# Two groups of resident blocks set one chunk earlier, and the rows ahead of their lists cleared

## The chip, the core and the metric

The kernel runs on one core of a Trainium2 chip. The metric is the time of one execution on the device in microseconds (us). The engines named here are PE (TensorE, matrix products), ACT (ScalarE), DVE (VectorE), POOL (GpSimd, which issues the indirect transfers here) and SP (SyncE, which issues the other transfers). Each engine works through its own instructions in a fixed order and waits on semaphores.

## The reference

A gated linear recurrence over four sequences of 3648 tokens with 256 features, and then a mixture of 16 experts, in four groups of four, over all 14592 tokens:

```python
a_t = np.exp(c * sig_r * np.log(a_base))           # c = 8
x_gated = sqrt(max(1 - a_t * a_t, 1e-6)) * sig_i * x
for t in range(S):
    h = a_t[:, t] * h + x_gated[:, t]
    y[:, t] = h
...
g_idx = argmax(y @ w_group)                        # the group, and then the expert in it
e_idx = argmax(y @ w_expert[g_idx])
out[tok] = g_w * e_w * (np.maximum(y @ w1[g, e], 0) @ w2[g, e])     # 256 -> 1024 -> 256
```

Each token goes through one expert only.

## The kernel before

**Recurrence and routing.** The tokens are worked off in 16 chunks (`SIZES`: 4, then thirteen times 8, then 4 and 2 tiles of 128 tokens), features on partitions. For each chunk six transfers on SP's queue bring the three inputs (`load`, L251), ACT forms the gates and the decay, DVE scales and scans (L359). PE then turns the chunk into rows and multiplies it with the routers in the same products (`rows1`, L366), and ACT copies them out (`rows2`, L372). DVE finds each token's expert (`route1`, `route3`, `weigh`). PE ranks the tokens within the experts (`rank`, L448 and L449), DVE turns the ranks into row numbers (`route4`), and POOL scatters the rows, with token number and weight beside the features, into a list for each expert in device memory (`scatter`, L469, one transfer for each tile of 128 tokens, into `y_s`). A list has room for `BPE` = 59 times 256 rows, and 384 rows (`HEAD`) lie before its first one. One block of 256 rows behind all lists stands for "nothing", and is cleared near the start by one transfer (`clear`, L313).

**The experts.** They are worked off in four kinds of steps:

- *Resident blocks* (`Block`): experts 0, 4, 8 and 12 (`RES`) have their weights loaded at the start (`load_raw`, L968, 2 MB each in two transfers). After the chunks named in `RSTAGES` (numbered from 0), PE sums the counts (`counts`, L598), and DVE decides for each of the four lists which 128 rows are taken (`near`, L690 to L707): they start at the smaller of (own count - 128) and the number already done; rows that were taken before, or precede the list, are masked. A group is then four blocks of 128 rows (`add_blocks`): a transfer of the rows on SP (`rows_block`, L479), two transposes on PE (`turn_block`, L1026), the masking of the columns on DVE (L485), a copy on ACT (`copy_block`, L1030), and two halves of first products (`mm1_block`, L1037, with `relu_block`, L1042, on ACT) and of second products (`mm2_block`, L1049; in f32 each product is two instructions in the trace, 32 and 16 for a block), then the weighting on DVE (L1054) and a scatter to the output by POOL (L1057).
- *Native units*: full blocks of 256 rows, found after the chunks 4, 7 and 10 (`STAGES`), 26 units in all. The first twelve (`NATIVE`) take their weights as they are, into the four places of the resident weights in turn (`load_native`, L976), and work in plain f32 (L982, L992, L1006).
- *Pair units*: the other units of 256 rows, the last 11 of them found after the last chunk. Their weights are split into two parts by ACT and DVE (L814, L816), and the products are made of three (L861, L930).
- *Tails*: one unit for each expert with the two or three blocks of 128 rows that are left.

Should there be more than 11 pairs after the last chunk, a conditional part at the very end takes the others one by one.

**The order.** Every step is an operation in a plan (`Plan`): engine, assumed cost, due time, what it follows, and the rings of buffers that it takes from. `Plan.run` places the operations on a modelled clock, the earliest first and among those the one that is due first, and emits the instructions in that order. So the order on each engine is fixed when the kernel is built. The due times of a block are those of its chunk plus `ORES` (60) and 7.2 for each block; the first unit's is that of the last of `RSTAGES` plus 60 and four times 7.2 (`first`, L1262); a chunk's due time is 16.5 times its number. A rank of a chunk follows the counts that were taken after the chunk before (`hold`). A transfer that reads rows from `y_s` waits for the scatters that stand before it in the order.

Of the kernel before, what the change touches and what calls it, by code (L numbers as in the profile page):

```python
# [8 lines left out]
F32 = mybir.dt.float32  # L9
# [35 lines left out]
class Plan:  # L45
# [14 lines left out]
    def op(self, engine, cost, emit, due, after=(), new=(), use=(), dma=0, table=None, soon=0.0, order=()):  # L60
        o = Op(engine, cost, emit, due, new, use, dma, table, soon)
        after = dict.fromkeys(a for a in after if a)
        order = dict.fromkeys(a for a in order if a and a not in after)
        o.wait = len(after) + len(order)
        for b in o.new + o.use:
            b.left += 1
        for a in after:
            a.then.append(o)
        for a in order:
            a.next.append(o)  # L70
        self.ops.append(o)
        return o
# [70 lines left out]
def rglru_moe_kernel(ctx: ExitStack, tc: tile.TileContext, x, r_gate, i_gate, a_param,  # L143
                     w_group, w_expert, w1, w2, out):
    nc = tc.nc
    V, S, G, T, DMA = nc.vector, nc.scalar, nc.gpsimd, nc.tensor, nc.sync

    P, NB = 128, 4
# [3 lines left out]
    NE = 16  # L152
# [3 lines left out]
    DW = D + LW  # L156
# [3 lines left out]
    TS = 256  # L160
    BPE = NTOK // TS + 2
    HEAD = 3 * P
# [1 line left out]
    SIZES = [4] + [8] * 13 + [4, 2]   # L164
    CH = 8

    RES, RSTAGES = (0, 4, 8, 12), (2, 3)
    STAGES = [(4, 8), (7, 9), (10, 9)]
    NATIVE = 12

# [1 line left out]
    PBUFS = dict(q_r=2, q_y=1, q_h=2, q_o=1)  # L172
    NA = sum(n for _, n in STAGES)
    NR = len(RES)
    assert NR == 4 and RSTAGES[-1] < STAGES[0][0]

    NP = NT >> 1
    NPS = 37 - NA
# [15 lines left out]
    const = ctx.enter_context(tc.tile_pool(name="const", bufs=1))  # L194
# [4 lines left out]
    rings, pools = {}, {}  # L199
# [13 lines left out]
    y_s = dram.tile([NBLK * TS, DW], F32, name="y_s")  # L213
# [13 lines left out]
    op = plan.op  # L227
# [77 lines left out]
        V.tensor_scalar(tcs[:, k:k + 1], tcol, float(k * P), None, op0=ALU.add)  # L305


    zero = const.tile([P, DW // 2], F32, name="zero")
    V.memset(zero, 0.0)

    def clear(dst):
        k = dst.shape[0] // P
        return DMA.dma_start(dst.rearrange("(p k) (a c) -> p (k a) c", k=k, a=2),  # L313
                             zero.unsqueeze(1).broadcast_to([P, 2 * k, DW // 2]))

    cleared = op("SP", 0.1, lambda: clear(y_s[NE * BPE * TS:, :]), 8.0, dma=5e5, soon=8)

# [1027 lines left out]
```

## Time and profile before

| | us |
|---|---|
| Median of three runs | 957.08 |
| Lowest and highest run | 954.96, 960.32 |
| The profiled execution | 946.03 |
| Its span, first to last instruction | 944.3 |

The profile is of one execution. Its page gives the busy time of each engine and, in 40 equal slices of the span, the busy tenths of each; other views cut the span into given stretches (busy time of each engine, the clock granted to PE, the busy share of the transfer engines), list one engine's instructions in order of time with the idle time before each and what ended it, or sum up who waited for whom. PEld is PE's loading of the stationary operand, which overlaps its products. "SPq" is SP issuing a transfer. Names such as `q_o<-w1l,hh` are the tile that is written and those that are read; weights and rows that share one place share its name.

### The profile page before, as it was taken

Reading aid. Unit: us, or ns where it says so; the run is one execution under the profiler, and the core shown is the slowest. Engines: PE = TensorE matmul, PEld = TensorE weight load, DVE = VectorE, ACT = ScalarE, POOL = GpSimd, SP = SyncE. Lnnn points to the kernel's source line nnn. Section 1 sums busy time; section 2 is a strip of 40 time slices with the busy share of each in tenths; the row PEclk is TensorE's granted clock in tenths of the full one; section 3 lists DMA queues with packets and bytes.
Section 4 is the critical chain, followed back from the end, with each engine's and each line's share of the span. In section 5 each row is a group of like instructions: output and inputs, shape, how many; then the busy total and the mean of one; then the engine's idle time right before and its main releaser. Section 6 shows DMA issues by size and latency. Waiting matters only on the chain. (4 is left out here: it accounts for less than half of the span.)

```text
span 944.3 us, 18467 instructions
## 1 busy us (share of the span) xinstructions
PE 856.5 (91%) x6082; PEld 821.6 (87%) x6082; DVE 620.2 (66%) x1304; ACT 590.5 (63%) x881; POOL 287.0 (30%) x290
## 2 busy tenths in 40 slices
PE   1335889999999999999999999999999999999984
PEld 1235879988989888999999999999999999999984
DVE  3779777675775426677777777777766666575761
ACT  9999889876797324555555555555645555454541
POOL 2244456465643653111111111111111312122222
PEclk9656889999999999999999999999999999999997
DMA  8997777889886756567667767777763657454410
GB/s 318 424 375 247 278 254 265 297 308 393 292 315 242 232 197 207 159 223 235 214 225 225 229 222 225 225 243 255 234 209 130 189 165 229 136 167 155 131 42 21
DMA packets 72456, 215.60 MB, mean 228 GB/s; under 512 B 10504, under 2 KB 28432, under 8 KB 68241
## 3 DMA queue, kind: packets, MB, share of 16 engines
q1 hardware_dynamic: 60464, 183.04, 58.1%
q0 software_dynamic: 11872, 31.10, 8.6%
q8 instruction: 59, 0.97, 0.4%
q14 instruction: 61, 0.49, 0.1%
HBM read 182.76 MB, written 33.43 MB: 229 GB/s over the span
## 5 line engine op out<-in xcount | busy, mean ns | idle before, releaser
L953 POOL DMA_INDIRECT out_dram<-o,cl x122 | 131.7, 1079 | 484.2 <-ACT o L945 286.1
L469 POOL DMA_INDIRECT y_s<-wf,pi x114 | 135.0, 1184 | 112.8 <-issue 71.4
L865 ACT ACTIVATE a<-q_h 128x384 fp32r<-128x384 f32 (+1 forms) x128 | 56.4, 447 | 108.5 <-PE q_h L861 92.8
L861 PE MATMUL q_h<-x,w1h 128*128 128x384 f32 (+1 forms) x512 | 116.1, 316 | 7.4 <-DVE i L868 6.8
L868 DVE SCALAR_TENSOR_TENSOR i<-q_h,a 128x384 fp32r<-128x384 f32 (+1 forms) x128 | 61.7, 497 | 85.3 <-ACT a L865 81.2
L865 ACT ACTIVATE hh<-q_h 128x512 fp32r<-128x512 f32 x100 | 60.3, 603 | 91.1 <-PE q_h L861 80.8
L861 PE MATMUL q_h<-xh,w1h 128*128 128x256 f32 x400 | 113.2, 283 | 0.0
L861 PE MATMUL q_h<-xl,w1h 128*128 128x256 f32 x400 | 112.6, 282 | 0.0
L861 PE MATMUL q_h<-xh,w1l 128*128 128x256 f32 x400 | 112.4, 281 | 0.0
L816 DVE TENSOR_TENSOR w1l<-wf,w1h 128x1024 fp32r<-128x1024 f32 x82 | 99.9, 1222 | 11.8 <-ACT w1h L814 9.8
L868 DVE SCALAR_TENSOR_TENSOR hl<-q_h,hh 128x512 fp32r<-128x512 f32 x100 | 68.9, 689 | 54.3 <-ACT hh L865 54.2
L366 PE MATMUL q_y<-yw,a 128*128 128x148 f32 x368 | 63.3, 318 | 41.2 <-DVE a L359 32.7
L366 PEld LDWEIGHTS q_y<-yw,a 128*128 128x128 f32 x368 | 57.5, 211 | 47.8 <-DVE a L359 18.8
L816 DVE TENSOR_TENSOR w2l<-wf,w2h 128x1024 fp32r<-128x1024 f32 x82 | 98.2, 1219 | 0.0
L861 PEld LDWEIGHTS q_h<-x,w1h 128*128 128x128 f32 x512 | 84.2, 188 | 9.0 <-issue 6.3
L814 ACT CAST w1h<-wf 128x1024 fp32r<-128x1024 f32 x82 | 86.9, 1064 | 0.3 <-issue 0.3
L814 ACT CAST w2h<-wf 128x1024 fp32r<-128x1024 f32 x82 | 83.9, 1043 | 0.0
L861 PE MATMUL q_h<-x,w1l 128*128 128x384 f32 (+1 forms) x256 | 79.7, 311 | 0.0
L861 PEld LDWEIGHTS q_h<-xh,w1h 128*128 128x128 f32 x400 | 75.3, 188 | 0.0
L861 PEld LDWEIGHTS q_h<-xh,w1l 128*128 128x128 f32 x400 | 75.3, 188 | 0.0
L861 PEld LDWEIGHTS q_h<-xl,w1h 128*128 128x128 f32 x400 | 75.2, 188 | 0.0
L359 DVE TENSOR_TENSOR_SCAN a<-a,v 128x1024 f32<-128x1024 f32 (+8 forms) x38 | 67.7, 1796 | 0.1
(341 smaller groups left out, 1930.6 us busy)
## 6 DMA issues: line engine op xcount, KB each, us to landing
wf<-in_moe_w_dram SPq DMA_DIRECT2D x164, 512.0 KB, 4.8
a<-in_r_gate_dram SPq DMA_DIRECT2D x26, 512.0 KB, 10.3
i<-in_i_gate_dram SPq DMA_DIRECT2D x26, 512.0 KB, 9.9
x<-in_x_dram SPq DMA_DIRECT2D x26, 512.0 KB, 8.8
g<-y_s SPq DMA_DIRECT2D x37, 276.0 KB, 4.1
w1h<-in_moe_w_dram SPq DMA_DIRECT2D x8, 1024.0 KB, 7.7
w1l<-in_moe_w_dram SPq DMA_DIRECT2D x8, 1024.0 KB, 9.8
w2h<-in_moe_w_dram SPq DMA_DIRECT2D x8, 1024.0 KB, 9.8
```

What stands on the lines that cost most here:

```text
L359: V.tensor_tensor_scan(a[:, sl], a[:, sl], v[:, sl], init, ALU.mult, ALU.add)
L366: T.matmul(q[:, k, h * P:h * P + YW], lhsT=ck.t["a", h][:, (2 * i + k) * P:(2 * i + k + 1) * P], rhs=yw[:, h, :], start=h == 0, stop=h == ...
L469: ins = G.indirect_dma_start(out=y_s, out_offset=bass.IndirectOffsetOnAxis(ap=ck.pi[:, k:k + 1], axis=0), in_=ck.t["yo", k // 4][:, k % 4, ...
L814: S.copy(hi[m.b][:, sl], src)
L816: V.tensor_tensor(lo[m.b][:, sl], src, hi[m.b][:, sl].bitcast(F32), op=ALU.subtract)
L861: T.matmul(q, lhsT=w[m.b][:, c, fs], rhs=mv[:, c, :N], start=n == 0, stop=n == 5)
L865: S.activation(hh, q, AF.Relu)
L868: V.scalar_tensor_tensor(hl, q, 0.0, hh.bitcast(F32), op0=ALU.max, op1=ALU.subtract)
L953: ins = G.indirect_dma_start(out=out, out_offset=bass.IndirectOffsetOnAxis(ap=m.col("idx", h), axis=0), in_=m.o[h], in_offset=None, bounds ...
```

## The change

The two groups of resident blocks follow the chunks 1 and 2 instead of 2 and 3. A list may now hold fewer than 128 rows when its first block is taken: the block then begins before the list's first row. The 128 rows before the four lists are therefore cleared, too. The zeros no longer have a small tile of their own in `const`, but take one of the two tiles into which units fetch their rows (`g`), for one row of 276 values on each partition; the clearing is now two transfers: one of 256 rows as before, with rows of 1104 bytes instead of halves of 552, and one of 4 x 128 rows. The plan is told 848 thousand bytes for it instead of 500 thousand. The due time of the first unit is taken from the last of `RSTAGES` and so becomes smaller by 16.5.

```diff
-    RES, RSTAGES = (0, 4, 8, 12), (2, 3)
+    RES, RSTAGES = (0, 4, 8, 12), (1, 2)
...
-    assert NR == 4 and RSTAGES[-1] < STAGES[0][0]
+    assert NR == 4 and RES == tuple(range(0, NE, NE // NR)) and RSTAGES[-1] < STAGES[0][0]
...
-    zero = const.tile([P, DW // 2], F32, name="zero")
+    zero = pools["g"].tile([P, 2, DW], F32, name="g")[:, 0:1, :]
     V.memset(zero, 0.0)
 
-    def clear(dst):
-        k = dst.shape[0] // P
-        return DMA.dma_start(dst.rearrange("(p k) (a c) -> p (k a) c", k=k, a=2),
-                             zero.unsqueeze(1).broadcast_to([P, 2 * k, DW // 2]))
-
-    cleared = op("SP", 0.1, lambda: clear(y_s[NE * BPE * TS:, :]), 8.0, dma=5e5, soon=8)
+    def clear():
+        k = TS // P
+        DMA.dma_start(y_s[NE * BPE * TS:, :].rearrange("(p k) c -> p k c", k=k), zero.broadcast_to([P, k, DW]))
+        heads = y_s[0:NE * BPE * TS, :].rearrange("(e r) c -> r e c", e=NR)[HEAD - P:HEAD]
+        DMA.dma_start(heads, zero.broadcast_to([P, NR, DW]))
+
+    cleared = op("SP", 0.1, clear, 8.0, dma=(2 + NR) * P * DW * 4, soon=8)
```

## The prediction

> **What bounds the kernel now.** First the page's shares and its 40 slices: which engine is full, and from when.
>
> ```profile
> span 944.3 us, 18467 instructions
> ...
> PE 856.5 (91%) x6082; PEld 821.6 (87%) x6082; DVE 620.2 (66%) x1304; ACT 590.5 (63%) x881; POOL 287.0 (30%) x290
> ...
> PE   1335889999999999999999999999999999999984
> ...
> ACT  9999889876797324555555555555645555454541
> ```
>
> A slice is 23.6 us. TensorE (PE) is full from the seventh on; before that ScalarE (ACT) is. So I cut the span by stage (columns: stretch, length, busy time and instructions of each engine, granted PE clock, DMA share, GB/s).
>
> ```profile
> 0.00:60.00 60.00, 20.16 (x84) 18.00 (x84) 33.74 (x79) 53.59 (x61) 14.09 (x27) 0.74 0.97 381
> ...
> 60.00:76.00 16.00, 2.17 (x9) 1.57 (x10) 14.41 (x31) 15.93 (x17) 12.26 (x11) 0.60 0.80 277
> 76.00:97.00 21.00, 13.62 (x58) 12.80 (x58) 18.95 (x42) 19.92 (x25) 6.72 (x7) 0.66 0.77 281
> 97.00:140.00 43.00, 37.44 (x233) 33.93 (x232) 31.23 (x94) 36.42 (x46) 22.10 (x23) 0.88 0.75 266
> 140.00:179.20 39.20, 39.13 (x274) 36.79 (x273) 31.48 (x67) 36.78 (x45) 19.51 (x15) 1.00 0.78 267
> 179.20:500.00 320.80, 320.80 (x2071) 297.87 (x2070) 200.35 (x520) 192.06 (x291) 123.81 (x129) 1.00 0.73 251
> 500.00:600.00 100.00, 100.00 (x846) 100.00 (x845) 72.78 (x110) 59.80 (x95) 16.06 (x17) 1.00 0.71 224
> 600.00:900.00 300.00, 293.41 (x2273) 291.67 (x2272) 201.47 (x334) 162.71 (x278) 62.98 (x55) 1.00 0.59 189
> ```
>
> From 140 us to 600 us PE stands idle for 0.07 us, at full clock. A microsecond won before 140 us therefore reaches the end whole, as long as PE never runs out of work behind it; one won on ACT or DMA there reaches it not at all. PE's idle time is 13.83 us in 60:76, 7.38 in 76:97 and 5.56 in 97:140, 26.8 in all.
>
> The timeline of PE shows what stands in these stretches (start, length, operation, count; in brackets the idle time before it).
>
> ```profile
> 54.65 0.22 PE L448 MATMUL q_y<-cn,tri 128*128 128x16 bf16 x1
> ...
> 68.94 0.17 PE L598 MATMUL q_y<-cacc,ones 128*128 128x16 bf16 x1 [2.44 <-DVE cacc L455]
> ...
> 76.73 2.18 PE L366 MATMUL q_o<-yw,a 128*128 128x148 f32 x8
> ...
> 90.78 0.60 PE L1026 MATMUL q_r<-yw,hl 128*128 128x128 f32 x4
> ...
> 97.05 5.54 PE L1037 MATMUL q_h<-xh,w1h 128*128 128x128 f32 x32
> ...
> 126.00 1.17 PE L366 MATMUL q_y<-yw,a 128*128 128x148 f32 x8
> ...
> 145.24 3.73 PE L1037 MATMUL q_h<-xh,w1h 128*128 128x128 f32 x32
> 148.81 1.17 PE L366 MATMUL q_y<-yw,a 128*128 128x148 f32 x8
> 149.82 3.62 PE L1049 MATMUL q_o<-w1l,hh 128*128 128x256 f32 x16
> ...
> 179.19 1.89 PE L992 MATMUL q_h<-xh,w1h 128*128 128x256 f32 x8
> ```
>
> The rank of the second chunk (L448) stands at 54.65, the counts for the first group (L598) at 68.94, behind the third chunk. Its first product (L1037) comes at 97.05; the eight blocks last until the first resident-weight unit (L992) at 179.19. One block is 3.73 + 3.62 = 7.35 us of PE at full clock, the eight 58.8 us.
>
> **The change part by part: the groups move.** The work per group stays the same; each group may begin one chunk sooner. How soon is read from the scatters, for which the row transfers (L479) wait.
>
> ```profile
> 67.30 2.02 POOL L469 DMA_INDIRECT y_s<-wf,pi  x1 [0.30 <-issue]
> ...
> 82.55 1.21 POOL L469 DMA_INDIRECT y_s<-wf,pi  x1 [0.30 <-issue]
> ```
>
> ```profile
> 85.31 1.95 SPq L479 DMA_DIRECT2D hl<-y_s  x2
> ...
> 140.54 1.55 SPq L479 DMA_DIRECT2D g<-y_s  x2
> ...
> 153.81 0.34 SPq L976 DMA_DIRECT2D w1l<-in_moe_w_dram  x1
> ```
>
> The third chunk's last scatter ends at 83.8 and the rows leave at 85.31; the second chunk's ends at 69.3, so its rows can leave at 70.8. From the row transfer to the first product it was 97.05 - 85.31 = 11.7 us before, of which 5.5 to the transposes (L1026); 70.8 + 5.5 is 76.3 for the transposes. PE can have block work from about 76. Nothing of 60:76 can be filled.
>
> How much of 76:97 is? What PE does there now is row products (L366):
>
> ```profile
> 76.00:97.00 21.00, 12.98 (x52) 12.08 (x51) 0.66 0.77 281
> ```
>
> I take the idle share and clock of 97:140, where blocks and row products mix already: 5.56/43 = 13%, clock 0.88. Then 21.0 - 2.7 = 18.3 us are busy; the row products take 12.98 x 0.66/0.88 = 9.7, the rest of what is there (13.62 - 12.98) 0.6. That leaves 8.0 us for blocks, 7.0 us at full clock. In 97:140 the first product ran cold, 5.54 against 3.73 us: with PE busy before it, and fewer such gaps later, I add 2 us. **Sum: 9 us** less between 76 and 179. Its bounds: 0, if no block fits in earlier; and, if every gap from 76 on closes at full clock, 7.38 + 13.62 x 0.34 + 5.56 + 37.44 x 0.12 = 22.1.
>
> The Trainium skill ("TensorE: Matmul & The Clock Gate", Part 1) says PE's clock is halved after an idle window of about 3.4 us and full after a busy one. The trace agrees: a group of eight row products takes 2.18 us at 76.73 and 1.17 at 126.00. By that rule alone all work from 76 on would be at full speed, and the sum would be 18.3 - 12.98 x 0.66 - 0.4 = 9.3 for 76:97 and 37.44 x 0.12 = 4.5 for 97:140, some 14 us.
>
> **Does the work last until unit 0 is ready?** At 179.2 - 9 = 170 the blocks end. Unit 0 needs its row numbers (140.54, where its rows are fetched) and its weights, issued at 153.81 when the first block of the second group let go of its place (149.82 + 3.62).
>
> ```profile
> w1l<-in_moe_w_dram SPq DMA_DIRECT2D x8, 1024.0 KB, 9.8
> ...
> y_s<-zero SPq DMA_DIRECT2D x1, 276.0 KB, 10.9
> ```
>
> They land 9.8 us later; with that block 9 us sooner, at 153.81 - 9 + 9.8 = 155. There are 15 us in hand, so the gap isn't merely moved.
>
> **ACT's and SP's share.** Each block gives ACT a copy and two relus (L1030, L1042), 0.38 + 2 x 0.59 = 1.6 us; eight are 12.5 us.
>
> ```profile
> L1042 ACT ACTIVATE hh<-q_h 128x512 f32<-128x512 f32 x16 | 9.2, 590 | 6.5 <-PE q_h L1037 6.1 <-PE q_y L598 0.4
> ...
> L1030 ACT COPY xh<-q_r 128x256 f32<-128x256 f32 x8 | 2.9, 380 | 0.3 <-PE q_h L1037 0.2
> ```
>
> Some of them precede the fifth chunk's counts already; at worst all 12.5 us move ahead of them and delay the row numbers by as much: 153, and the weights 9.8 later, 163, still inside the 170. SP's transfers of the rows go past chunk loads; the number of these transfers is the same, and they wait earlier.
>
> ```profile
> SPq L479 <- DMA y_s<-wf,pi: 11.9, 2, 6.1
> ```
>
> The Trainium skill ("DMA: Bandwidth & Descriptors", Anatomy of one DMA) says that a DMA's wait is served on the issuing sequencer before dispatch. That speaks against the change: loads behind the row transfer stand still. The row above agrees (two waits, 6.1 us the longest). By that rule alone the 9 us would shrink by up to 6.1, if ACT ran out of loaded chunks in such a wait.
>
> **The clearing.** It sends 276 KB for the last block as before and 4 x 128 rows of 1104 bytes more, 565 KB; at the 381 GB/s of 0:60, where DMA is full, 1.5 us of transfer. It delays loads, not PE; between 0 (loads run ahead of ACT) and 1.5 us I take 0, because block work covers it. A second issue on SP costs some 0.7 us there. The zeros move into a work tile that is free until 140 us: nothing.
>
> **The rows taken.** Counting the reference's router on its inputs through the kernel's own tables, the groups take 936 rows before and 814 after: lists of 75 to 168 rows don't always fill 128. The 122 others fall to later units. The pairs left at the end stay 11, which is what the program holds, and the last units with three blocks stay 9. The trace has 9 x 8 = 72 relus of that form:
>
> ```profile
> L865 ACT ACTIVATE a<-q_h 128x384 fp32r<-128x384 f32 x72 | 35.5, 494 | 69.8 <-PE q_h L861 54.5 <-issue 5.8 <-PE q_y L930 5.4
> ```
>
> So this costs nothing. A twelfth pair would cost at least 96 products at 100/846 us, a load of 4.8 and a split: an estimate of 18 us.
>
> **The rivals.**
> 1. *Nearly full filling.* The planner finds block work for most gaps from 76 on and the clock stays up: 13 to 22 us, about 940. For it: 97:140 and 140:179 had no shortage once blocks were there. Against: orders are fixed, and 5.56 us of gaps stayed with blocks at hand.
> 2. *The planner doesn't bring the first products forward by much* (PE's fixed order keeps row products, and their waits, ahead): within 4.8 us either way, 955. For it: the copies and relus compete on an ACT that is 95% busy in 76:97 (19.92 of 21).
> 3. *Slower: the fifth chunk is late.* Place: ACT's fixed order. A relu waits there for a cold product, with the next chunks' work behind it.
>
> ```profile
> ACT hh L1042 <- PE q_h L1037: 5.7, 3, 2.3
> ```
>
> If all eight relus of the first group wait 2.3 us (18.4), ACT's own 12.5 us come on top and SP waits 6.1 us more, unit 0's row numbers slip 37 us to 178 and its weights come at 187, 8 us after the old start: 965. It decides from a slip of 29 us (179.2 - 9.8 - 140.5). Against it: the waits before were three.
>
> **How the numbers follow.** The profiled execution took 946.03 us around its span of 944.3; minus 9 is 937. It lies 11 below the median of the runs, 957.08; I take the difference over to that: **948 us**. About 0.5%, 4.8 us, is what a measurement of this kernel can tell from no change. Chances: forecast (5 to 13 us won, 944 to 952) 0.45; rival 1 0.25; rival 2 0.19; rival 3, with all else that is slower, 0.11. Faster 0.70, same 0.19, slower 0.11. The range is 935, at the full 22 us, to 959; it leaves out rival 3 and the worse half of rival 2's far side.
>
> **What would show it.** Counts (L598) for the first group at 56 to 60 and the first L1037 at 76 to 84 instead of 97; PE's busy time in 76:97 near 18 us; the first L992 near 170 with no idle time ahead of it; PE full from there to 600; a second L313-like issue ahead of 10 us. An L992 that waits for weights or for L479 speaks for rival 3; an L1037 still at 95 for rival 2. I am wrong altogether if the last units change in number or shape, or PE's clock in the full stages does.

## The result, and the profile after

The changed kernel takes **941.36 us** (median of four runs, 938.15 to 942.80); the kernel before, run beside it, takes 956.70 (954.96 to 960.32). The ratio is 0.9844, with a 95% interval of 0.9815 to 0.9873: faster by 1.3 to 1.9%. The profiled execution of the changed kernel took 940.21 us around a span of 938.5, where that of the kernel before took 946.03 around 944.3. So the runs differ by 15.3 us and the two profiles by 5.8. Why these numbers are so far apart is one of the questions below.

All line numbers behind the change are one higher than before (L367 for L366, L1038 for L1037, and so on). First the page's shares and slices:

```profile
span 938.5 us, 18448 instructions
...
PE 850.7 (91%) x6082; PEld 812.7 (87%) x6082; DVE 619.4 (66%) x1304; ACT 590.3 (63%) x881; POOL 287.1 (31%) x290
...
PE   1337988999999999999999999999999999999984
...
ACT  8889989588699233556555555556545455454641
```

PE has the same 6082 instructions, but is busy for 5.8 us less. PE's idle time is the span less its busy time, 87.8 us in both profiles. All of the 5.8 us therefore stands under "busy"; of the idle time nothing went on balance. The stages show why (columns as in the prediction):

```profile
60.00:76.00 16.00, 2.95 (x13) 2.13 (x13) 13.64 (x36) 15.02 (x17) 11.81 (x13) 0.61 0.75 267
76.00:97.00 21.00, 18.90 (x125) 17.73 (x126) 19.82 (x42) 20.86 (x27) 9.31 (x9) 0.87 0.74 260
97.00:140.00 43.00, 40.01 (x277) 36.30 (x277) 31.29 (x89) 40.06 (x52) 27.06 (x23) 1.00 0.75 270
140.00:179.20 39.20, 36.51 (x223) 33.14 (x222) 33.05 (x69) 30.65 (x38) 15.42 (x14) 1.00 0.88 334
179.20:500.00 320.80, 315.38 (x2055) 291.29 (x2054) 200.87 (x524) 199.05 (x299) 125.31 (x129) 1.00 0.72 250
500.00:600.00 100.00, 100.00 (x846) 100.00 (x846) 73.44 (x112) 58.98 (x93) 17.80 (x18) 1.00 0.70 224
```

From 60 to 140 PE now idles 13.05 + 2.10 + 2.99 = 18.1 us, where it was 26.8: 8.6 less. From 140 to 500 it idles 2.69 + 5.42 = 8.1 us, where it was 0.07. **Between these two profiles, what was filled in front has come back behind.** The granted clock rose from 0.66 to 0.87 in 76:97 and from 0.88 to 1.00 in 97:140, and the same products take less busy time at the higher clock.

The timeline of PE answers to the one shown of before:

```profile
59.68 0.22 PE L599 MATMUL q_y<-cacc,ones 128*128 128x16 bf16 x1
...
84.90 3.74 PE L1038 MATMUL q_h<-xh,w1h 128*128 128x128 f32 x32
...
149.08 0.17 PE L449 MATMUL q_y<-cn,tri 128*128 128x16 bf16 x1 [0.99 <-DVE cn L423]
...
150.70 0.66 PE L983 MATMUL q_r<-yw,g 128*128 128x128 f32 x4 [1.43 <-DMA g<-y_s]
...
163.97 1.89 PE L993 MATMUL q_h<-xh,w1h 128*128 128x256 f32 x8
```

The counts come at 59.68, the first block product at 84.90 instead of 97.05, and the first unit's first product at 163.97 instead of 179.19. That is 15 us earlier, but gaps of 0.3 to 1.4 us stand ahead of it now. The waits of PE in 140:500 name what ends such gaps:

```profile
PE q_y L367 <- ACT wf L373: 2.1, 2, 1.5
PE q_y L449 <- DVE cn L423: 1.7, 2, 1.0
PE q_r L983 <- DMA g<-y_s: 1.4, 1, 1.4
```

PE waits for the row copies of ACT, the ranks of DVE and fetched rows: for all that feeds it, and for no single one. Before, it was the other way round. These are ACT's waits in 140:400, first of the kernel before and then of the changed one:

```profile
ACT wf L372 <- PE q_y L366: 17.4, 16, 2.2
```

```profile
ACT wf L373 <- PE q_y L367: 4.6, 5, 2.2
...
ACT wf L373 <- DMA y_s<-wf,pi: 2.7, 1, 2.7
```

Sixteen times a copy waited for PE's row products; now five do, and one waits for a scatter to release the tile that it writes (`wf`). I read this so: PE was behind with its work before; now it has nearly caught up with its suppliers.

### The profile page after: what moved, and what is told of

Read it like the earlier page. It is cut to its first block, busy times and chain, and to the rows that moved or that the text cites. A ratio compares the mean times of both kernels' runs of the same rounds, so it can differ in the third digit from the quotient of the medians.

```text
span 938.5 us, 18448 instructions
## 1 busy us (share of the span) xinstructions
PE 850.7 (91%) x6082; PEld 812.7 (87%) x6082; DVE 619.4 (66%) x1304; ACT 590.3 (63%) x881; POOL 287.1 (31%) x290
## 4 chain that ended last, share of the span: by engine, by line
PE 74%; issue 5%; DVE 4%; ACT 3%; DMA 2%; POOL 1%; another core or an unknown queue 0%; DVEq 0%; SPq 0%; POOLq 0%; ACTq 0%
PE q_h L862 25%; PE q_o L931 22%; PE q_h L993 7%; PE q_o L1007 7%; PE q_y L367 4%; PE q_y L931 3%; PE q_r L838 2%; PE q_h L1038 1%; PE q_o L1050 1%; DMA out_dram<-o,cl 1%; POOL y_s L470 1%; DMA g<-y_s 1%; DMA y_s<-wf,pi 1%; POOL out_dram L954 1%; ACT wf L373 1%
## 5 line engine op out<-in xcount | busy, mean ns | idle before, releaser
L367 PE MATMUL q_y<-yw,a 128*128 128x148 f32 x368 | 61.7, 312 | 42.8 <-DVE a L360 28.1
L367 PEld LDWEIGHTS q_y<-yw,a 128*128 128x128 f32 x368 | 55.5, 205 | 51.4 <-issue 16.5
```

Source lines behind the costliest of these rows:

```text
L367: T.matmul(q[:, k, h * P:h * P + YW], lhsT=ck.t["a", h][:, (2 * i + k) * P:(2 * i + k + 1) * P], rhs=yw[:, h, :], start=h == 0, stop=h == ...
```

## The experiments

Three chips took part. The kernel before takes 943.96 us on chip A (26 runs), 944.95 on chip C (17 runs) and about 956 on chip B (955.55 in 17 runs, 956.65 in 12). On chip B it also spreads from 946 to 959.

For the comparison of profiles I count the instructions that PE has done by 500 us. Every complete kernel has 6082, and around 500 us all of them work on pair units at 846 in 100 us (the row of 500:600), so 8.46 more at that point are 1 us of lead.

### What changes with the chip

The kernel before, unchanged, on chip A.

> The kernel before, unchanged, profiled once more: its profiled execution (946.03 us) lay 11 us under the median of its runs, while the change's lay on its own median. Theory A, the two profiles show the change as it is: this profile has a span near 944 again and no idle PE time from 140 to 600 us. Theory B, the usual execution of the kernel before has a loss that the first profile missed: a span of 952 to 958, with the difference in PE's idle time or in the granted clock of one stretch. Time: ratio 1.000 to the kernel before by both.

Measured: ratio 0.9996 (0.9983 to 1.0010), median 944.12, span 941.0; PE idles 26.6 us in 60:140 and not at all in 140:500. So this chip gives the picture and the time of the first profile. The 957 us of the first runs fit chip B; which chip they ran on is not recorded. The transfers in the first profile of before carry landing times, as on A and C; in the profile of after they carry none, as on B. So the two profiles very likely are from two chips. To have both kernels from one chip, each was profiled again on chip B, in one comparison, with no edit:

> The kernel before, unchanged, for its profile on this chip: on one chip it took 944 us and on another 946 to 960. If the chip is of the second kind: a span of 950 or more, with the difference to the first profile either in idle PE time between 140 and 500 us (row copies that wait for scatters, as in the change) or in the granted clock and the stretch before 140. Ratio 1.000.

> The change, unchanged, beside the four on one chip. Ratio to the kernel before 0.985 to 0.999 by what was seen so far; where the kernel before takes 944 (first kind of chip) 0.994 to 0.999, where it takes 955 (second kind) 0.984 to 0.992. Idle PE time between 140 and 500 us 8 to 10 us.

Measured on chip B: the kernel before 953.95 (ratio 0.9983, 0.9952 to 1.0013), the changed one 941.55 (0.9884, 0.9823 to 0.9945). Earlier on the same chip the unchanged change had this text and result:

> The change itself, unchanged, beside the kernel before on the same chip. The kernel before took 944 us in the last runs and 957 in those that the change was first compared with, while the change's own runs (938 to 943) may have come from either kind of chip. Theory A, the gain of 1.6% is the change's and holds everywhere: ratio 0.980 to 0.988. Theory B, most of it was the difference of two chips, and the change is worth what the two profiles show (5.8 us of span, 0.6%): ratio 0.992 to 0.998.

Measured: 944.40, ratio 0.9895 (0.9846 to 0.9944). On chip B the change is worth 0.5 to 1.8% in both comparisons. Stretches of the two profiles, before and then after:

```profile
76.00:97.00 21.00, 13.58 (x57) 12.76 (x58) 19.09 (x35) 20.00 (x25) 7.37 (x8) 0.66 0.78 282
97.00:140.00 43.00, 34.71 (x202) 31.31 (x201) 29.66 (x90) 34.30 (x44) 21.52 (x22) 0.82 0.69 239
...
0.00:140.00 140.00, 71.57 (x346) 64.00 (x347) 96.05 (x233) 122.86 (x143) 53.49 (x66) 0.73 0.84 309
0.00:500.00 500.00, 426.53 (x2619) 391.45 (x2620) 321.52 (x816) 347.03 (x469) 196.73 (x208) 0.92 0.75 266
```

```profile
76.00:97.00 21.00, 18.95 (x116) 18.15 (x117) 18.62 (x41) 19.84 (x27) 10.21 (x9) 0.78 0.72 235
97.00:140.00 43.00, 39.55 (x280) 35.95 (x278) 30.68 (x89) 39.15 (x50) 26.47 (x23) 1.00 0.77 279
...
0.00:140.00 140.00, 80.92 (x483) 73.54 (x483) 96.75 (x243) 126.54 (x150) 58.21 (x68) 0.82 0.85 313
0.00:500.00 500.00, 433.38 (x2754) 397.99 (x2755) 331.58 (x833) 357.61 (x486) 204.89 (x210) 0.95 0.77 274
```

By 500 us the changed kernel has done 135 instructions more, 16.0 us of lead, and its span is 17.0 shorter (938.9 against 955.9; the medians of the runs lie 12.4 apart, so this pair shows more than the usual difference). At 140 us the lead is 137 instructions already (483 against 346): on this chip it reaches 500 us almost whole. Here DVE and ACT are further, too, by 500 us (833 and 486 instructions against 816 and 469); both kernels on chip A stand at 833 and 486. The 17.0 are 7.6 us less idle (11.3 less in 60:140, 2.5 more in 140:500, 1.2 more elsewhere) and 9.4 less busy (861.6 to 852.2). The clock in two rows accounts for most of the 9.4: 13.58 x (1 - 0.66/0.78) + 34.71 x (1 - 0.82) = 8.3 us, an estimate. On this chip the kernel before is worse off in 97:140 than on the others: 34.71 us busy at 0.82, where the first profile has 37.44 at 0.88. ACT does 44 instructions there, against 46, and the transfers move 239 GB/s against 266. What holds it back is open: the traces of chip B carry no landing times of transfers.

### One part at a time

The clearing alone, with the groups where they were, on chip A:

```diff
-    RES, RSTAGES = (0, 4, 8, 12), (1, 2)
+    RES, RSTAGES = (0, 4, 8, 12), (2, 3)
```

> The change with the groups left behind the third and fourth chunk: only the larger clearing and the zeros' place are new. My step (565 KB more, hidden): 955 to 958 us, ratio 0.998 to 1.003. Rival (the clearing delays the first loads and the delay reaches the end): 1.5 to 3 us more, ratio 1.002 to 1.004.

Measured: 946.67, ratio 1.0016 (1.0000 to 1.0033). The clearing costs 0 to 3 us, 1.5 in the middle, and can't be told from nothing; it was costed at 0, with 1.5 as the upper bound.

The groups and the clearing, without the earlier due time of the first unit:

```diff
-    first = cks[RSTAGES[-1]].due + ORES + NR * STEPB
+    first = cks[RSTAGES[-1] + 1].due + ORES + NR * STEPB
```

> The change with the units' due times left where they were: the groups follow the second and third chunk, and the first unit stays due one chunk later. If the gain comes from the blocks filling PE's gaps before 140 us: about the whole of it, 938 to 945 us. If it comes from the units' earlier place in the order: 952 to 957. If the idle time of 8 us that the change shows between 140 and 500 us comes from units that stand too early in the order: 933 to 938, with less than 3 us of it left.

> The groups moved and the units' due times left, once more: on the chip where the kernel before takes 944 us it made no difference (ratio 1.0002), and the whole change made 1.1% on the chip where the kernel before takes 954 to 957. If the kernel before takes over 950 here: theory A, the moved groups are the cause and the chips differ in what the kernel before loses (its row copies waiting for scatters): ratio 0.984 to 0.993, the time near the change's 941 to 945. Theory B, the units' earlier due times are needed for it: ratio 0.997 to 1.003. If the kernel before takes 944 here: ratio 0.999 to 1.002 again, and the question stays open.

Measured on chip A 943.52, ratio 1.0002 (0.9990 to 1.0014), and on chip C 943.27, ratio 0.9989 (0.9977 to 1.0000): no difference that counts. Here the trace is plainest. Both kernels on chip A, before and then with the groups moved:

```profile
0.00:140.00 140.00, 74.24 (x400) 67.39 (x401) 99.10 (x248) 128.42 (x150) 55.60 (x67) 0.78 0.86 319
0.00:500.00 500.00, 434.24 (x2746) 402.45 (x2747) 332.66 (x833) 357.46 (x486) 198.95 (x210) 0.94 0.77 273
```

```profile
0.00:140.00 140.00, 80.13 (x490) 72.96 (x491) 98.32 (x244) 128.78 (x152) 59.60 (x68) 0.83 0.86 314
0.00:500.00 500.00, 431.66 (x2751) 398.68 (x2752) 334.48 (x833) 358.05 (x486) 199.41 (x210) 0.95 0.77 274
```

At 140 us PE is 90 instructions ahead; at 500 us it is 5 ahead. **The whole lead is gone in between.** DVE and ACT stand at 833 and 486 in both rows of 0:500: by this count the chunks and their routing have come no further. Between the two marks PE idles 8.5 us on chip A and 6.9 on chip C, against none in the kernel before on chip A (it was not profiled on C). Half of it or more is one wait of 4.2 us, the same on both chips. From the timelines of PE and ACT on chip A:

```profile
214.56 3.78 PE L1007 MATMUL q_o<-w1l,hh 128*128 128x256 f32 x8 [4.23 <-ACT o L946]
```

```profile
210.67 1.28 ACT L339 ACT_TABLE_LOAD   x1
211.96 2.19 ACT L339 ACTIVATE v<-v,la 128x1024 f32<-128x1024 f32 x2
214.06 0.45 ACT L946 ACTIVATE o<-q_o,cl 128x256 f32<-128x256 f32 x1
```

These are the third unit's second products. They write `q_o`, of which there is one tile (`PBUFS`), and wait until ACT has copied out its half of the unit before (L946). ACT is busy without a gap from 206.44 on, mostly with the gates of a chunk, and comes to the copy at 214.06. The unit's weights (`w1l`) were issued at 196.27 and landed 9.2 us later, so it wasn't them. PE had caught up with ACT's fixed order.

The due time alone, in the kernel before:

```diff
-    first = cks[RSTAGES[-1]].due + ORES + NR * STEPB
+    first = cks[RSTAGES[-1] - 1].due + ORES + NR * STEPB
```

> The kernel before with only the units' due times 16.5 us earlier, the groups where they were. If blocks in PE's gaps are the cause: no gain, 954 to 960 us, since PE has nothing else to do there. If the units' place in the order is the cause: 941 to 946.

Measured on chip A: 951.63, ratio 1.0072 (1.0056 to 1.0089), with 5.9 us idle in 140:500. So the units' earlier place by itself costs time; why is not shown. I take it that they stand in front of work that was ready. Whether the due time gains something together with the earlier groups isn't settled: the whole change was profiled and repeated on chip B only, the groups without it on A and C only.

### Why the first product comes at 84.9

In the changed kernel the rows of the first group leave late:

```profile
80.63 1.55 SPq L480 DMA_DIRECT2D hl<-y_s  x2
```

```profile
69.30 2.02 POOL L470 DMA_INDIRECT y_s<-wf,pi  x1 [0.30 <-issue]
...
78.13 0.98 POOL L470 DMA_INDIRECT y_s<-wf,pi  x1 [0.31 <-issue]
```

The scatter at 78.13 is of the third chunk, which these rows don't need; it stands ahead of them in the order, and a transfer that reads `y_s` waits for all scatters ahead of it. The next kernel puts the row transfers ahead of the scatters that are added later (`ga` is the operation of the transfer):

```diff
+    fetched = []
...
-                      use=[b["pi"], yos[k // 4]], dma=2 * P * DW * 4) for k in range(0, K, 2)]
+                      use=[b["pi"], yos[k // 4]], dma=2 * P * DW * 4, order=list(fetched)) for k in range(0, K, 2)]
...
+            fetched.append(ga)
```

> The change, with the scatters of later chunks put behind the row transfers of the groups in the order (one line: they follow them). In the change the first group's rows wait for a scatter of the third chunk (they leave at 80.6 us; the second chunk's last scatter ended at 71.3), and the second group's last row transfer waits 11 us for one of the fourth chunk, with the loads behind it. If that wait is what keeps the blocks from starting at 76: rows at 72 to 73, first product (L1039 here) at 75 to 80 instead of 84.9, 3 to 6 us less than the change. If PE's gaps there are set by ACT and by PE's own order: the same time as the change within 2 us.

Measured on chip B: 951.66, ratio 0.9980 (0.9947 to 1.0014), so 7 us slower than the change in the same comparison. That was a miss. The rows leave 8 us earlier than in the change beside it (81.19 there), and the first product moves by less than 2 (86.66 there, 86.02 in the other profile of the change on this chip); of the two timelines, SP's and PE's:

```profile
73.22 1.62 SPq L480 DMA_DIRECT2D hl<-y_s  x2
```

```profile
80.66 2.34 PE L367 MATMUL q_y<-yw,a 128*128 128x148 f32 x8 [1.00 <-ACT wf L373]
82.80 1.06 PE L1029 MATMUL q_r<-yw,hl 128*128 128x128 f32 x4
...
84.92 3.73 PE L1040 MATMUL q_h<-xh,w1h 128*128 128x128 f32 x32
```

PE's fixed order keeps the fourth chunk's row products ahead of the transposes, and these wait for ACT. What holds the first product is that order, not the rows alone. And PE idles 15.3 us in 140:500 instead of 9.8 in the change that ran beside it, 8.0 of them in row products that wait for ACT's copies (three waits, 5.8 the longest). Before the longest, ACT itself stands still for 3.8 us; PE's, ACT's and SP's timelines:

```profile
191.82 2.34 PE L367 MATMUL q_y<-yw,a 128*128 128x148 f32 x8 [5.82 <-ACT wf L373]
```

```profile
188.28 1.06 ACT L343 ACTIVATE i<-i 128x1024 f32<-128x1024 f32 x1 [3.78 <-DMA i<-in_i_gate_dram]
```

```profile
173.94 0.40 SPq L480 DMA_DIRECT2D g<-y_s  x1
...
176.03 0.43 SPq L251 DMA_DIRECT2D i<-in_i_gate_dram  x1
```

The gate input (`i`) that ACT waits for was issued on SP behind a fetch of rows, and such fetches wait there for scatters (35.2 us in 160:192, in three waits). So here a chunk's inputs came late. Whether that is what the edit costs as a whole isn't shown.

### What the idle time behind 140 us waits for

Only the first group one chunk earlier, the second where it was:

```diff
-    RES, RSTAGES = (0, 4, 8, 12), (1, 2)
+    RES, RSTAGES = (0, 4, 8, 12), (1, 3)
```

> The change with only the first group moved (second and fourth chunk; the units' due times as before). If the gain comes from the gaps of 76 to 97 us, which only the first group reaches: PE is as busy there as with the change (19 us), and the time lies within 2 us of the change or under it, since the gap behind the blocks (140 to 164 us) closes. If both groups are needed: within 2 us of the kernel before.

Measured on chip B: 964.77, ratio 1.0107 (1.0050 to 1.0163): slower than before, against what was expected. PE idles 24.4 us in 60:140 and 22.5 in 140:500. The waits of PE and then of ACT in its trace:

```profile
PE q_y L367 <- ACT wf L373: 14.1, 3, 7.8
```

```profile
ACT wf L373 <- DMA y_s<-wf,pi: 6.8, 3, 5.9
```

Three times the row products stand still until ACT has copied out the ones before them. The stop of 5.4 us at 277.98 follows a copy on ACT that waits 5.9 us for a scatter to empty a tile; what ACT waits for ahead of the longest, 7.8 us, the trace doesn't name. I take it that a half-done move leaves the fixed orders of PE, ACT and POOL worse matched than either whole.

Two kernels leave work out, to see whether the idle time is one of transfer rate or of POOL's queue. Without the loads of the native units' weights (they work with what stands in the four places):

```diff
-        if i == 0:
...
-        DMA.dma_start(m.w[i], m.src[i])
+        m.w = raw[m.u % NR]
```

> The change, with the twelve native units' weight loads left out (24 MB between 140 and 320 us; they work with the weights that lie there, so their rows are not the experts'). The change shows 8 to 10 us of idle PE time between 140 and 500 us that the kernel before doesn't have. Theory D, the transfer engines are too slow there, for weights, chunks and scatters: that idle time falls under 3 us, 4 to 8 us less than the change. Theory Q, it is the fixed order of POOL and ACT (a row copy waits for a buffer that a scatter must empty, and the scatter stands behind output scatters): 5 us or more of it stays, within 4 us of the change.

Without the scatters of the native units' results:

```diff
+        if m.native:
+            return
```

> The change, with the output scatters of the twelve native units left out on POOL (24 transfers of 128 KB; their rows of the output stay unwritten). Theory Q: the scatters of the chunks no longer stand behind them, the row copies (L373) wait less for their buffers, the idle time of PE between 140 and 500 us falls from 8 to 10 us to under 4, and the time is 3 to 7 us less than the change's. Theory D: 3 MB less in all, 5% of what moves there, so the idle time and the time stay within 2 us of the change's.

Measured on chip B, beside the change at 941.55 (ratio 0.9884, 0.9823 to 0.9945): without loads 939.72, ratio 0.9849 (0.9791 to 0.9907); without output 937.45, ratio 0.9829 (0.9767 to 0.9890). The row of 140:500 in the change, without the loads, and without the output:

```profile
140.00:500.00 360.00, 352.46 (x2271) 324.45 (x2272) 234.83 (x591) 231.07 (x337) 146.68 (x143) 1.00 0.73 259
```

```profile
140.00:500.00 360.00, 352.45 (x2255) 324.98 (x2256) 234.96 (x597) 228.88 (x334) 142.08 (x143) 0.99 0.56 187
```

```profile
140.00:500.00 360.00, 354.30 (x2288) 327.31 (x2288) 235.68 (x594) 231.22 (x338) 114.10 (x119) 1.00 0.72 251
```

With 187 GB/s instead of 259 the idle time is the same 7.5 us, which speaks against the rate of the transfers as its cause. With POOL's work reduced by 33 us it is 5.7 us: POOL's queue may be a part of it, and a smaller one than was expected. The unedited change has 7.5, 8.1 and 9.8 us there in its three profiles, so 5.7 lies below all three, but by less than the 2.3 that they differ by. The two intervals overlap that of the change, so this part rests on the idle time in one profile each. A larger ring of `wf` tiles, which would test it more directly, wasn't tried. The rest, some 5.7 us, is spread over waits of 0.3 to 1.6 us, and is not settled by any run.

## Why the prediction was right, and where not

The forecast was 948 us, from 9 us gained; the runs gave 941.4, from 15.3 us. That lies inside the range of 935 to 959, but outside the band of 944 to 952 that had a chance of 0.45. That the range held is in part luck: more was gained in front than the sum had, part of it was lost again behind, and the difference between profile and runs didn't stay. Point by point:

- **The groups come forward: right.** Counts at 59.68 (56 to 60 forecast); 18.90 us busy in 76:97 ("near 18"); a clock of 0.87 there (0.88 assumed). The stretch 76:97 by line, the blocks' first products (L1038), their second products (L1050) and the row products (L367):

```profile
76.00:97.00 21.00, 5.73 (x49) 5.70 (x50) 0.87 0.74 260
```

```profile
76.00:97.00 21.00, 3.78 (x16) 2.90 (x16) 0.87 0.74 260
```

```profile
76.00:97.00 21.00, 9.77 (x54) 8.89 (x54) 0.87 0.74 260
```

  That is 5.73 + 3.78 = 9.5 us for the blocks, where 8.0 were forecast, and 9.77 for the row products, where it was 9.7.
- **When the rows leave: wrong.** "its rows can leave at 70.8" overlooked that the third chunk's scatters stand ahead of the transfer: 80.63. The first product at 84.90 lies just behind the forecast 76 to 84. It cost little: with the rows at 73.22 the product came at 84.92.
- **The size of the clock's share: too small.** I added 2 us to the filled time for the clock and the cold product. PE's busy time fell by 5.8 us between the two profiles, by 9.4 on chip B, and by 3.1 on chip A with the groups alone (854.2 to 851.1); the kernel before by itself differs by 2.3 between its first profile and that of chip A. This is the term of the sum that was mis-sized. The clock-gate rule of the Trainium skill ("TensorE: Matmul & The Clock Gate", Part 1) was given 14 us by itself in the prediction. The 8.6 us of idle time filled in 60:140 and the 5.8 of busy time make 14.4, which is near it; the trace agrees with full speed in 97:140 (a clock of 1.00), but in 76:97 the clock was 0.87, and the row products at 78.73 still took 2.18 us.
- **"A microsecond won before 140 us therefore reaches the end whole, as long as PE never runs out of work behind it": its condition failed.** It does run out: 8.1 us idle in 140:500 against 0.07, though "PE full from there to 600" was forecast. I tested the condition on one point, the weights of unit 0, and there it held: no wait for them stands ahead of the first L993, which came at 163.97, even before the 170. But blocks done early are no longer there as a backlog behind which small waits of PE pass unseen; the turned waits between ACT and PE, the lead of 90 instructions that shrinks to 5 on chip A, and the 4.2 us behind ACT's gates there speak for this reading. So between the two profiles 8.6 + 5.8 us were gained, 8.1 given back, and some 0.5 lost elsewhere: 5.8, not 9. On chip B, in contrast, the whole change keeps its lead (137, then 135); the kernel before stands idle for 5.0 us in 140:500 there, too, and is behind in DVE's and ACT's work. Whether the chip or the units' due time makes this difference is open.
- **From the profile to the runs: not a constant.** I carried the 11 us between the profiled execution and the median over unchanged. They go with the chip, as far as three chips show, and the change doesn't leave them as they are: the changed kernel takes 942 and 944 us on chip B (medians), where the kernel before takes 954 to 957. This very likely is why the runs gained 15.3 us and the profiles 5.8. What the whole change does on a chip where the kernel before takes 944 us was not run; without the due time it does nothing there.
- **SP's longer wait: no cost seen.**

```profile
SPq L480 <- DMA y_s<-wf,pi: 26.1, 3, 14.3
```

  Three waits, 14.3 us the longest, twice what I had allowed for; yet ACT is busy for 75.9 us in 60:140, where it was 72.3. The loads were far enough ahead there. Rival 3 had no part in it.
- **Clearing and tails: right within their bounds.** The clearing alone lies 1.5 us up (0 to 3), at its upper bound; the tails have 72 relus of three blocks, as before. How many rows the groups take no run shows.

```profile
L866 ACT ACTIVATE a<-q_h 128x384 fp32r<-128x384 f32 x72 | 35.6, 494 | 69.7 <-PE q_h L862 54.5 <-PE q_y L931 5.7 <-issue 5.5
```

- **Rivals.** The first (13 to 22 us, about 940) came nearest to the time, but only half by its own cause: the clock stayed up, as it said, while 5.1 of the 12.9 us of gaps in 76:140 stayed; the rest is very likely the chip. The second fell with the first product at 84.90.

## What to carry to other kernels

Before a gain at the front of a kernel is counted in full, ask how far each supplier of the bounding engine is ahead of it: compare how much work that engine has done at a late mark (here at 500 us), not only how idle it is where the change acts. A filled gap can pay twice, in idle time and in clock, so the busy time belongs in the sum too. And take the profile and the times of both kernels from one chip: here the same edit is worth 1.1% on one chip, and the part of it that ran on two others was worth nothing there. Over all fourteen profiles the span falls as ACT's count of instructions at 500 us rises, from 461 at 965.2 us to 488 at 935.5; this shows how far the kernel is as a whole, not what holds it, since the units' relus are in that count.

## What the runs showed of the hardware

The kernel before takes 944 and 945 us on two chips (medians) and 954 to 957 on a third, and its runs on the third spread by 13 us, those on the others by 3 to 6. The changed kernel, of which runs on a known chip are on the third only, takes 939 to 948 there. PE's granted clock is higher where its work is denser: 0.60 to 0.61 at 13 to 18% busy (60:76), 0.66 at 65% (76:97 before), 0.82 to 0.95 at 81 to 87% (97:140 before), 0.78 to 0.87 at 90% (76:97 after) and 1.00 at 92 to 93% (97:140 after). The busy share alone doesn't set it: with the groups alone 76:97 has 0.81 on chip A and 0.91 on C, both at 95%. A cut of the transfers in 140:500 from 259 to 187 GB/s left PE's idle time as it was, in one profile each.
